# Banded attention and a mixture of experts in one kernel: larger loads of the plain heads, dealt out over the steps; half of the V shifts on VectorE; another opening; another PSUM pool for routing

## The chip, the cores and the metric

The kernel runs on one core of a Trainium2 chip. The metric is the device time of one execution in microseconds (us). Three runs of the kernel before gave 720.86, 727.56 and 734.02 us; their median is 727.56 us.

## The reference

```python
B, H, S, D = 8, 8, 576, 64          # batch, heads, sequence, head size
# attention: window 32; heads 0-3 "plain", heads 4-7 dilated by 4
rel = pos[:, None] - pos[None, :]
mask_plain = (rel >= 0) & (rel < 32)
mask_dil   = (rel >= 0) & (rel < 128) & (rel % 4 == 0)
attn = softmax(where(mask, q @ k.T / 8, -1e9));  out = attn @ v
x = out.transpose(0, 2, 1, 3).reshape(B * S, H * D)      # 4608 tokens x 512
# mixture of experts: one of 8 experts a token
logits = x @ w_gate + modality_bias[modality_id]
e = argmax(logits);  g = softmax(logits)[e]
out = g * (relu(x @ w1[e]) @ w2[e])                      # w1: 512 x 1024, w2: 1024 x 512
```

All data are float32.

## The kernel before

The kernel has two parts. The first runs over the eight batch elements ("batches" here) and computes attention and routing. The second, `slots`, runs the experts over slots of up to 256 tokens.

**Units and steps.** A batch is cut into nine units of 64 queries for each of four (head, block) pairs. Work is a software pipeline of 72 + 6 steps, written out by hand as the body of one loop over `t`; TensorE, VectorE, ScalarE and SyncE run in the order in which that code is written (`manual_schedule`), GpSimd in an order that is tied down too. A step is called b.m here: batch b, m-th step of the batch (t = 9b + m). Step t does, in this order: the scores of unit t and, on VectorE, mask and maximum (`sm`, `nmx`; GpSimd then subtracts); the exponential of unit t-1; one shift of V (`shift_v`, L148); the transposes of the probabilities of unit t-2 and of the result rows of unit t-5; one "chunk" of transposes that turn the next Q and K (`qk_chunks`, L332 for plain heads, L339 for dilated ones); probabilities times V of unit t-3 (`attend`, L427) and its normalisation on VectorE, which ends in the tile `x_sb` (L445); the gate logits of the unit before that; then, twice, a stage of the background tasks (`advance`), of which `gating` is the routing of a batch; then the store of finished `x_sb` to the DRAM tensors `x_dram` (`keep`, L458 to L468); and last the loads for later batches.

**What waits for what.** `x_sb` has three buffers, each filled by two units and freed when its store has landed. PSUM pool `o` has two buffers of one bank, from which `attend`, the logits and both matmul groups of `gating` (L549: turning the logits; L574 to L577: counting ranks) take turns. PSUM pool `two` has two buffers of two banks (`pw`) for all transposes.

**SyncE's queue.** All plain loads and stores are issued by SyncE, one after the other. In step b.2 it gets the loads of the next batch's plain K, in b.3 those of plain Q and dilated V, in b.7 dilated Q and K of the batch after, in b.8 plain V. `load_one` (L115) stages plain heads with six tokens of 64 a row on 2 x 48 rows: a DMA for each of four heads and two halves, eight for K and eight for Q, 73.7 KB each (48 rows x 6 tokens x 256 B). Stores go between them: one in each of b.1, b.3, b.5, b.7, three in b.8.

**Shifts.** The V tiles hold each block of 64 keys; their first 32 rows are the last 32 of the block before, copied on chip by `shift_v`: eight copies of 32 x 520 numbers a batch, in steps b.0 to b.7, all on ScalarE.

**Routing.** `gating` of batch b starts in step 5 of the batch after. For batch 2 it is followed by `slot_info`, by `fetch_slot` (loads of token lists, `idt`, L743) and by gathers on GpSimd (`xr`, L313, the helper line of all GpSimd work); these fill four early slots, so that the experts can start when the last unit's scores are done.

**Opening.** The first loads, before the loop, are put in order by a scheduler. Nine dummy matmuls (L180) run while they are under way.

Of the kernel before, what the change touches and what calls it, by code (L numbers as in the profile page):

```python
# [10 lines left out]
F32 = mybir.dt.float32  # L11
# [3 lines left out]
AF = mybir.ActivationFunctionType  # L15
# [3 lines left out]
ET = mybir.EngineType  # L19
# [8 lines left out]
WIN = 32  # L28
NCLS = 4
CL = S // NCLS  # L30
TQ = 64
# [3 lines left out]
PG = 64  # L35
SI = S // (2 * PQ)
GB = 96
NGB = S // GB
# [21 lines left out]
def kernel(  # L60
# [46 lines left out]

    def load_one(b, kd, src, queue=nc.sync):

        t = ald.tile([PG + PQ, SI * 4 * D], F32, name="st")  # L110
        if kd == 0:
            tv = t.rearrange("p (s h d) -> p s h d", h=4, d=D)
            for h in range(4):
                for e in range(2):
                    queue.dma_start(out=tv[PG * e:PG * e + PQ, :, 2 * (h % 2) + h // 2],  # L115
                                    in_=src[b, h].rearrange("(e p s) d -> e p s d", e=2, s=SI)[e])
            return tv
        tv = t.rearrange("p (h x) -> p h x", h=4)
        for e in range(2):
            queue.dma_start(out=tv[PG * e:PG * e + PQ], in_=by_parity(src, b)[e])  # L120
        return tv

    def load_qk(b, kd, queue=nc.sync):
        kn = load_one(b, kd, k)
        return load_one(b, kd, q, queue), kn

# [3 lines left out]
    def load_v(b, kd, part=slice(None)):  # L130

        t = vw(b, kd)
        if kd == 0:
            for a in range(2):
                nc.sync.dma_start(out=t[WIN:KW, 0:2 * NTILE, 1 + D * a:1 + D * (a + 1)],
                                  in_=v[b, 2 * a:2 * a + 2].rearrange("g (i p) d -> p (g i) d", p=TQ))
        else:
            vv = v[b, 4:8].rearrange("h (j c a) d -> c j h (a d)", c=2, a=2)
            for i, o, c, j, n in VPARTS[part]:
                nc.sync.dma_start(out=t[WIN + o:WIN + o + n, 4 * i:4 * i + 4, 1:1 + 2 * D], in_=vv[c, j:j + n])  # L140
        return t

    def shift_v(b, kd, n):

        t = vw(b, kd)
        i = NTILE * (n % 2) + 4 * (n // 2) if kd == 0 else 4 * n
        o = i + 1 if kd == 0 else i + 4
        nc.scalar.copy(out=t[0:WIN, o:o + 4].rearrange("p i d -> p (i d)"), in_=t[TQ:KW, i:i + 4].rearrange("p i d -> p (i d)"))  # L148

    first = [ald.tile([PG + PQ, SI * 4 * D], F32, name="st").rearrange("p (h x) -> p h x", h=4) for _ in range(2)]  # L150
    for n in range(SI // 2):
        for t, src, queue in zip(first, (q, k), (nc.scalar, nc.sync)):
            xs = slice(2 * D * n, 2 * D * (n + 1))
            for e in range(2):
                queue.dma_start(out=t[PG * e:PG * e + PQ, :, xs], in_=by_parity(src, 0)[e, :, :, xs])
    state = {('qk', 0, 1): tuple(first)}
    warm = cpool.tile([P, 512], BF16, name="warm")
# [9 lines left out]
    nc.vector.memset(hot, 0.0)  # L167
    nc.scalar.activation(out=hot, in_=hot, func=AF.Exp)
# [3 lines left out]
    state['v', 0, 1] = load_v(0, 1, slice(0, 2))  # L172
    state['qk', 0, 0] = load_qk(0, 0)
    load_v(0, 1, slice(2, None))
    state['v', 0, 0] = load_v(0, 0)
    ident = cpool.tile([P, P], F32, name="ident")
    make_identity(nc, ident)
    for _ in range(NWARM):
        pw = psum['o'].tile([P, 512], F32, name="po")
        nc.tensor.matmul(out=pw, lhsT=warm[:, 0:P], rhs=warm, start=True, stop=True)  # L180

# [142 lines left out]
    def qk_chunks(kd, qn, kn):  # L324


        def turn(n, src, is_q, pt):
            if kd == 0:
                for i in range(SI):
                    for e in range(2):  # L330
# [3 lines left out]
                return [((qT[0] if is_q else kT[0][:, :, WIN:])[:, n].rearrange("c (e x) -> c e x", e=2), pt[:, :, 0:SI * PQ])]  # L334
            off = 0 if is_q else 4 * PQ
            for h in range(4):
                for e in range(2):
                    rows = slice(PG * e, PG * e + PQ)
                    nc.tensor.transpose(out=pt[:, e, off + PQ * h:off + PQ * (h + 1)], in_=src[rows, h, 2 * D * n:2 * D * (n + 1)],  # L339
                                        identity=ident[rows, rows])  # L340
# [711 lines left out]
    for ch in qk_chunks(1, *state['qk', 0, 1]):  # L1052
        ch()
    state['qk', 1, 1] = load_qk(1, 1)

# [17 lines left out]
    for t in range(NU + LAG):  # L1073
# [12 lines left out]
        if t < NU:  # L1086
            if m == 0:
                state['lT', b] = gwk.tile([2 * LGP, S], F32, name="lT")
            if b + 1 < B:
                if m == 4:  # L1090
                    pieces = qk_chunks(1, *state['qk', b + 1, 1])
                elif m == 8:
                    pieces = qk_chunks(0, *state['qk', b + 1, 0])
            units.append(Unit(b, m0, [state['v', b, 0], state['v', b, 1]], state['lT', b]))
            units[t].scores()
        step()
# [19 lines left out]
        for x in kept:  # L1116
            x.keepT()
        for _ in range(2 if t == 3 else 1):
            if pieces:
                pieces.pop(0)()  # L1120
        step()

# [17 lines left out]
        if 0 <= t - 4 < NU:  # L1140
            units[t - 4].keep(nc.sync)
        if t < NU and b + 1 < B:

            if m == 2:
                state['k', 0] = load_one(b + 1, 0, k)
            elif m == 3:
                state['qk', b + 1, 0] = load_one(b + 1, 0, q), state['k', 0]
                state['v', b + 1, 1] = load_v(b + 1, 1)
            elif m == 7 and b + 2 < B:
                state['qk', b + 2, 1] = load_qk(b + 2, 1)  # L1150
            elif m == 8:
                state['v', b + 1, 0] = load_v(b + 1, 0)
        advance([*round_of, B - 1] if moe and t < NU else range(-1, B))
# [42 lines left out]
```

## Time and profile before

| | |
|---|---|
| runs | 720.86, 727.56, 734.02 us |
| profiled execution | 715.86 us; span of its trace 714.1 us |
| first mask of unit 0, first of batch 1, first of batch 7 | 13.41, 48.47, 231.45 us |
| first matmul of the experts | 260.09 us |
| TensorE, VectorE, ScalarE, GpSimd busy | 652.5, 478.5, 440.3, 251.8 us |

The times of the third and fourth row are starts from the span's beginning. The expert part, from 260 us on, keeps TensorE busy almost without a gap (100.00 of the 100 us from 500 to 600). The text below looks at the part ahead of it. A row of a table by stretches has: the stretch, its length, then for each engine the busy time and the number of its instructions, then the granted TensorE clock (1.00 is full), the mean busy share of the 16 DMA engines, and GB/s. A row of the timeline has start, duration, engine (a q behind it: its instruction queue, here DMA issues), line, operation, tiles, shape, count, and in brackets the idle time of the engine before it with what ended it.

### The profile page before, as it was taken

The numbers are of one execution on the slowest core, as the hardware profiler recorded it, in microseconds if no ns is written. First come the engines' busy times: TensorE is split into PE (matmuls) and PEld (weight loads), VectorE is DVE, ScalarE is ACT, GpSimd is POOL, SyncE is SP. The second block draws the span as 40 slices with busy tenths as digits, with TensorE's granted clock in tenths as the row PEclk, the third lists the DMA queues.
The fourth block names the chain that finished last, engine by engine and source line by source line (L and its number), as shares of the span: only waits on it lengthen the run. The fifth ranks groups of instructions, "written<-read, shape, count | busy, mean of one in ns | idle before, by whom it ended". The sixth has DMA issues, their size and how long they took to land. (4 is left out here: it accounts for less than half of the span.)

```text
span 714.1 us, 19778 instructions
## 1 busy us (share of the span) xinstructions
PE 652.5 (91%) x7237; PEld 566.8 (79%) x7237; DVE 478.5 (67%) x1165; ACT 440.3 (62%) x917; POOL 251.8 (35%) x322
## 2 busy tenths in 40 slices
PE   6698788796887989999999999999999999999994
PEld 4587677675765868888998989989999999989983
DVE  4277477676666666796667766676677766677662
ACT  4479589585866655555665666556655656656652
POOL 6223456344655554343332313332233322211110
PEclk9999699778889669999999999999999999999997
DMA  6885867858686961389594324862333315941460
GB/s 150 161 200 135 192 170 155 197 127 181 157 187 161 252 155 54 88 150 265 136 258 139 99 81 116 242 174 72 96 87 104 118 69 130 242 137 59 122 168 12
DMA packets 136327, 103.45 MB, mean 145 GB/s; under 512 B 68800, under 2 KB 114386, under 8 KB 136228
## 3 DMA queue, kind: packets, MB, share of 16 engines
q1 hardware_dynamic: 126804, 82.31, 47.2%
q0 software_dynamic: 8176, 19.26, 9.2%
q8 instruction: 58, 0.95, 0.6%
q10 hardware_dynamic: 1248, 0.59, 0.3%
q14 instruction: 41, 0.34, 0.2%
HBM read 127.52 MB, written 29.39 MB: 220 GB/s over the span
## 5 line engine op out<-in xcount | busy, mean ns | idle before, releaser
L989 PE MATMUL pt<-xh,w1l 128*128 128x256 f32 (+1 forms) x608 | 172.5, 284 | 2.8 <-DVE w1l L938 2.8
L989 PE MATMUL pt<-xh,w1h 128*128 128x256 f32 (+1 forms) x608 | 173.3, 285 | 1.0 <-ACT w1h L937 0.9
L989 PE MATMUL pt<-xl,w1h 128*128 128x256 f32 (+1 forms) x608 | 171.9, 283 | 0.0
L995 ACT ACTIVATE hh<-pt 128x256 fp32r<-128x256 f32 (+1 forms) x152 | 57.5, 379 | 155.6 <-PE pt L989 155.6
L938 DVE TENSOR_TENSOR w2l<-w2q,w2h 128x512 fp32r<-128x512 f32 x152 | 104.9, 690 | 45.5 <-ACT w2h L937 37.9
L989 PEld LDWEIGHTS pt<-xh,w1h 128*128 128x128 f32 x608 | 115.9, 191 | 9.7 <-ACT w1h L937 3.0
L313 POOL DMA_INDIRECT xr<-x_dram,idt x74 | 82.1, 1110 | 112.9 <-DMA x_slot<-xr 64.3
L989 PEld LDWEIGHTS pt<-xl,w1h 128*128 128x128 f32 x608 | 115.9, 191 | 5.9
L989 PEld LDWEIGHTS pt<-xh,w1l 128*128 128x128 f32 x608 | 116.4, 191 | 4.3 <-DVE w1l L938 4.3
L969 PE MATMUL py<-w2h,hh 128*128 128x512 f32 x296 | 118.7, 401 | 0.0
L969 PE MATMUL py<-w2h,hl 128*128 128x512 f32 x296 | 116.7, 394 | 0.0
L969 PE MATMUL py<-w2l,hh 128*128 128x512 f32 x296 | 115.5, 390 | 0.0
L996 DVE SCALAR_TENSOR_TENSOR hl<-pt,hh 128x256 fp32r<-128x256 f32 (+1 forms) x152 | 63.0, 415 | 76.0 <-ACT hh L995 75.9
L313 POOL DMA_INDIRECT out_dram<-ys,idt x37 | 40.4, 1091 | 200.4 <-ACT ys L972 120.6
L938 DVE TENSOR_TENSOR w1l<-w1q,w1h 128x512 fp32r<-128x512 f32 x152 | 104.4, 687 | 7.8 <-ACT w1h L937 7.7
L937 ACT CAST w1h<-w1q 128x512 fp32r<-128x512 f32 x152 | 94.6, 622 | 8.6 <-DMA w1q<-in_moe_w_dram 8.2
L937 ACT CAST w2h<-w2q 128x512 fp32r<-128x512 f32 x152 | 93.1, 612 | 0.0
L313 POOL TENSOR_TENSOR sm<-sm,nmx 128x384 f32<-128x384 f32 x72 | 60.0, 833 | 85.5 <-DVE nmx L397 43.8
L969 PEld LDWEIGHTS py<-w2l,hh 128*128 128x128 f32 x296 | 55.6, 188 | 13.8
L427 PE MATMUL po<-vw,pT 96*64 96x65 f32 (+1 forms) x1216 | 63.6, 253 | 0.4 <-DVE x_sb L445 0.4
L969 PEld LDWEIGHTS py<-w2h,hh 128*128 128x128 f32 x296 | 56.2, 190 | 7.7 <-issue 0.7
L969 PEld LDWEIGHTS py<-w2h,hl 128*128 128x128 f32 x296 | 55.6, 188 | 5.8
(178 smaller groups left out, 976.4 us busy)
## 6 DMA issues: line engine op xcount, KB each, us to landing
w2q<-in_moe_w_dram SPq DMA_DIRECT2D x76, 512.0 KB
w1q<-in_moe_w_dram SPq DMA_DIRECT2D x152, 256.0 KB
x_slot<-xr SPq DMA_DIRECT2D x18, 512.0 KB
xg<-x_slot SPq DMA_DIRECT2D x72, 128.0 KB
x_dram<-x_sb SPq DMA_DIRECT2D x32, 256.0 KB
vw<-in_v_dram SPq DMA_DIRECT2D x16, 288.0 KB
st<-in_k_dram SPq DMA_DIRECT2D x64, 72.0 KB
st<-in_q_dram SPq DMA_DIRECT2D x64, 72.0 KB
```

What stands on the lines that cost most here:

```text
L313: ins = tc.keep_in_program_order(getattr(nc.gpsimd, name)(*args, **kw))
L427: nc.tensor.matmul(out=pov[r0:r0 + nr, g, cs], lhsT=self.pT[:, 2 * g + a, r0:r0 + nr], rhs=self.vts[kd][:, blk, cs], start=True, stop=True)
L937: nc.scalar.copy(out=hi, in_=raw)
L938: nc.vector.tensor_tensor(out=lo, in0=raw, in1=hi.bitcast(F32), op=ALU.subtract)
L969: nc.tensor.matmul(out=py[u], lhsT=ht[:, us], rhs=wt, start=(f + n == 0), stop=(f + n == FC + 1))
L989: nc.tensor.matmul(out=ph, lhsT=wt[:, c, :], rhs=xt[:, c, 0:cols], start=(c + i == 0), stop=(c + i == KC + 1))
L995: nc.scalar.activation(out=hh, in_=ph, func=AF.Relu)
L996: nc.vector.scalar_tensor_tensor(out=hl, in0=ph, scalar=0.0, in1=hh.bitcast(F32), op0=ALU.max, op1=ALU.subtract)
```

## The change

**Plain heads.** They are staged with nine tokens a row on 64 rows, one head of a pair in the upper and one in the lower half of the partitions: a DMA a head, four for K and four for Q, 147.5 KB each. `turn` transposes 64 x 128 blocks: 10 in a first chunk and 8 in a second, for K and for Q, 36 a batch where there were 48. ScalarE's copy out of PSUM then writes runs of five or four numbers instead of one long run.

**Loads dealt out.** From batch 1 on the loads are issued in parts of one to three DMAs a step: K in b.0 and b.1, Q in b.2 and b.3, dilated V in b.3 to b.5, dilated K in b.6, dilated Q in b.7 and b.8, plain V in b.8 and the next step.

**Shifts.** Those with an odd number go to VectorE (steps b.1, b.3, b.5, b.7).

**Routing.** `loose()` takes a buffer of pool `two` where no chunk is left in the step (`state['loose']`), and one of pool `o` otherwise. The counting of ranks moves on by one background stage.

**Opening.** The order of its loads is fixed by hand: dilated Q and K, all of dilated V, plain K and Q, plain V. 21 more dummy matmuls (`fill`), of 64 rows, stand between the first chunks and units.

```diff
-    def load_one(b, kd, src, queue=nc.sync):
-        t = ald.tile([PG + PQ, SI * 4 * D], F32, name="st")
-        if kd == 0:
-            tv = t.rearrange("p (s h d) -> p s h d", h=4, d=D)
-            for h in range(4):
-                for e in range(2):
-                    queue.dma_start(out=tv[PG * e:PG * e + PQ, :, 2 * (h % 2) + h // 2],
-                                    in_=src[b, h].rearrange("(e p s) d -> e p s d", e=2, s=SI)[e])
-            return tv
...
+    def load_plain(t, b, src, heads, queue=nc.sync):
+        tv = t[:, 0:SP * 2 * D].rearrange("p (s a d) -> p s a d", a=2, d=D)
+        for h in heads:
+            queue.dma_start(out=tv[PG * (h % 2):PG * (h % 2 + 1), :, h // 2], in_=src[b, h].rearrange("(p s) d -> p s d", s=SP))
...
-        nc.scalar.copy(out=t[0:WIN, o:o + 4].rearrange("p i d -> p (i d)"), in_=t[TQ:KW, i:i + 4].rearrange("p i d -> p (i d)"))
+        move = nc.vector.tensor_copy if n % 2 else nc.scalar.copy
+        move(out=t[0:WIN, o:o + 4].rearrange("p i d -> p (i d)"), in_=t[TQ:KW, i:i + 4].rearrange("p i d -> p (i d)"))
...
+    with tc.manual_schedule(engines={ET.SP, ET.Activation}):
+        state['qk', 0, 1] = staged(), staged()
+        for xs in (slice(0, 2 * D), slice(2 * D, None)):
+            load_dil(state['qk', 0, 1][0], 0, q, range(2), xs, nc.scalar)
+            load_dil(state['qk', 0, 1][1], 0, k, range(2), xs)
+        nc.scalar.activation(out=hot, in_=hot, func=AF.Exp)
+        state['v', 0, 1] = load_v(0, 1)
...
+    def fill(n):
+        po = psum['o'].tile([P, 512], F32, name="po")
+        for _ in range(n):
+            nc.tensor.matmul(out=po, lhsT=warm[0:PG, 0:P], rhs=warm[0:PG], start=True, stop=True)
...
-                for i in range(SI):
-                    for e in range(2):
-                        rows = slice(PG * e, PG * e + PQ)
-                        nc.tensor.transpose(out=pt[:, e, i:SI * PQ:SI], in_=src[rows, i, 2 * n:2 * n + 2].rearrange("p a d -> p (a d)"),
+                s0, ns = (0, 5) if n == 0 else (5, SP - 5)
+                for i in range(ns):
+                    for g in range(2):
+                        rows = slice(PG * g, PG * (g + 1))
+                        nc.tensor.transpose(out=pt[:, g, i:ns * PG:ns], in_=src[rows, 2 * D * (s0 + i):2 * D * (s0 + i + 1)],
...
+    def loose():
+        if psum['two'] and state['loose']:
+            return psum['two'].tile([P, 2, 512], F32, name="pw")[:, 0]
+        return psum['o'].tile([P, 512], F32, name="po")
...
-        lgp = psum['o'].tile([P, 512], F32, name="po")
+        lgp = loose()
...
-        rkp = psum['o'].tile([P, 512], F32, name="po")
+        if b < B - 1:
+            yield
+        rkp = loose()
...
+        state['loose'] = not pieces
         for _ in range(2 if t == 3 else 1):
             if pieces:
                 pieces.pop(0)()
...
+            if m == 0 and b > 0:
+                load_v(b, 0, slice(1, 2))
+            if b + 1 < B:
...
+                if m < 4 and b > 0:
+                    load_plain(state['qk', b + 1, 0][m < 2], b + 1, k if m < 2 else q, (2 * (m % 2), 2 * (m % 2) + 1))
...
+                if 3 <= m < 6:
+                    state['v', b + 1, 1] = load_v(b + 1, 1, slice(2 * (m - 3), 2 * (m - 2)))
```

**SyncE, third batch.** In the queue before, from the store of step 2.1 to the loads of step 2.7 (`st` is the staging tile of Q and K, `vw` V, `x_sb` a finished result; the shapes are rows x tokens x numbers):

```order
L465 DMA x_dram_84<-x_sb 128x2x256
L115 DMA st<-in_k_dram 48x6x64 x8
L465 DMA x_dram_84<-x_sb 128x2x256
L115 DMA st<-in_q_dram 48x6x64 x8
L140 DMA vw_104<-in_v_dram 64x4x128 x2
L140 DMA vw_104<-in_v_dram 16x4x128
L140 DMA vw_104<-in_v_dram 48x4x128
L140 DMA vw_104<-in_v_dram 64x4x128
L140 DMA vw_104<-in_v_dram 32x4x128
L468 DMA x_dram_85<-x_sb 128x2x256 x2
L120 DMA st<-in_k_dram 48x4x384 x2
```

The same place after the change, from step 2.0 to step 2.5:

```order
L116 DMA st<-in_k_dram 64x9x64 x2
L469 DMA x_dram_84<-x_sb 128x2x256
L116 DMA st<-in_k_dram 64x9x64 x2
L116 DMA st<-in_q_dram 64x9x64 x2
L469 DMA x_dram_84<-x_sb 128x2x256
L116 DMA st<-in_q_dram 64x9x64 x2
L137 DMA vw_104<-in_v_dram 64x4x128 x2
L137 DMA vw_104<-in_v_dram 16x4x128
L137 DMA vw_104<-in_v_dram 48x4x128
L472 DMA x_dram_85<-x_sb 128x2x256
L137 DMA vw_104<-in_v_dram 64x4x128
L137 DMA vw_104<-in_v_dram 32x4x128
```

Between the store of step 2.3 (the second of the `x_dram_84` rows) and that of step 2.5 (`x_dram_85`) there were fourteen loads and are now six.

**TensorE, steps 1.6 and 1.8 after the change.** First the turning of the logits (`lT`), then the counting of ranks (`oh`, `upper`), each with what stands ahead of it:

```order
L343 MATMUL pw<-ident,st 128x48 x16
L431 MATMUL po<-vw_106,pT 64x65 x8
L512 MATMUL po<-ux,wgs 64x128 x2
L558 MATMUL po<-ident,lT 96x72 x6
L396 MATMUL pss<-kT_102,qT_100 64x96 x8
```

and, two steps on,

```order
L335 MATMUL pw<-ident,st 128x64 x10
L431 MATMUL po<-vw_104,pT 64x65 x8
L512 MATMUL po<-ux,wgs 64x128 x2
L585 LDWEIGHTS upper
L585 MATMUL po<-oh,upper 96x48
```

Both still write `po`, pool `o`, behind `attend` and the logits as before: a chunk (L343, L335) was waiting at the head of both steps, so `state['loose']` was false. The same holds for the batches after it, but for one group, L558 of batch 6 in step 7.6, which writes `pw`.

**GpSimd, steps 4.8 to 5.1.** Before (`xr` is a gather of rows by the list `idt`, `table` a scatter, `t_...` and `run` small routing operations):

```order
L313 TENSOR_TENSOR run<-run,r_3660 96x8 x3
L313 TENSOR_TENSOR t_3657<-t_3657,oh 96x48
L313 TENSOR_TENSOR sm<-sm,nmx 128x384
L601 DMA table<-pay,dst 41472x3
L313 DMA xr<-x_dram_84,idt 128x256
L313 TENSOR_TENSOR sm<-sm,nmx 128x384
L313 DMA xr<-x_dram_85,idt 128x256
```

After:

```order
L315 TENSOR_TENSOR run<-run,r_3575 96x8 x3
L315 TENSOR_TENSOR sm<-sm,nmx 128x384
L315 TENSOR_TENSOR t_3572<-t_3572,oh 96x48
L612 DMA table<-pay,dst 41472x3
L315 TENSOR_TENSOR sm<-sm,nmx 128x384
L315 DMA xr<-x_dram_84,idt 128x256
L315 DMA xr<-x_dram_85,idt 128x256
```

The first gather now stands one subtraction (`sm`), that is one step, later, and the routing product `t` behind the subtraction instead of ahead of it.

More of the change, by code (lines that the diff above doesn't have):

```diff
@@ L36 @@
 SI = S // (2 * PQ)
+SP = S // PG
 GB = 96
@@ L133, in load_v @@
         if kd == 0:
-            for a in range(2):
+            for a in range(2)[part]:
                 nc.sync.dma_start(out=t[WIN:KW, 0:2 * NTILE, 1 + D * a:1 + D * (a + 1)],
@@ L147, in shift_v @@
         o = i + 1 if kd == 0 else i + 4
[L148 to L156, printed above, removed]
+        move = nc.vector.tensor_copy if n % 2 else nc.scalar.copy
+        move(out=t[0:WIN, o:o + 4].rearrange("p i d -> p (i d)"), in_=t[TQ:KW, i:i + 4].rearrange("p i d -> p (i d)"))
     warm = cpool.tile([P, 512], BF16, name="warm")
@@ L167 @@
     nc.vector.memset(hot, 0.0)
-    nc.scalar.activation(out=hot, in_=hot, func=AF.Exp)
     for kd in (1, 0):
@@ L171 @@
     nc.vector.memset(kT[1][:, :, WIN + HP:], 0.0)
[L172 to L175, printed above, removed]
+    state = {}
+    with tc.manual_schedule(engines={ET.SP, ET.Activation}):
[5 more added lines that the diff above has]
+        state['v', 0, 1] = load_v(0, 1)
+        state['qk', 0, 0] = staged(), staged()
+        load_plain(state['qk', 0, 0][1], 0, k, range(4))
+        load_plain(state['qk', 0, 0][0], 0, q, range(4))
+        state['v', 0, 0] = load_v(0, 0)
     ident = cpool.tile([P, P], F32, name="ident")
     make_identity(nc, ident)
-    for _ in range(NWARM):
-        pw = psum['o'].tile([P, 512], F32, name="po")
-        nc.tensor.matmul(out=pw, lhsT=warm[:, 0:P], rhs=warm, start=True, stop=True)
+    def fill(n):
+        po = psum['o'].tile([P, 512], F32, name="po")
+        for _ in range(n):
+            nc.tensor.matmul(out=po, lhsT=warm[0:PG, 0:P], rhs=warm[0:PG], start=True, stop=True)
+    fill(NWARM)
     starts = [None, 0, CL - 2 * TQ]
@@ L338, in turn @@
                     rows = slice(PG * e, PG * e + PQ)
-                    nc.tensor.transpose(out=pt[:, e, off + PQ * h:off + PQ * (h + 1)], in_=src[rows, h, 2 * D * n:2 * D * (n + 1)],
+                    nc.tensor.transpose(out=pt[:, e, off + PQ * h:off + PQ * (h + 1)], in_=src[rows, SI * D * h + 2 * D * n:SI * D * h + 2 * D * (n + 1)],
                                         identity=ident[rows, rows])
@@ L1053 @@
         ch()
-    state['qk', 1, 1] = load_qk(1, 1)
+        fill(3)
+    state['qk', 1, 1] = staged(), staged()
+    load_dil(state['qk', 1, 1][1], 1, k, range(2))
+    load_dil(state['qk', 1, 1][0], 1, q, range(2))
     credit = 0.0
@@ L1094 @@
             units.append(Unit(b, m0, [state['v', b, 0], state['v', b, 1]], state['lT', b]))
+            if t in (1, 2):
+                fill(2)
             units[t].scores()
@@ L1120 @@
                 pieces.pop(0)()
+        if t < 4:
+            fill(2)
         step()
@@ L1141 @@
             units[t - 4].keep(nc.sync)
[L1142 to L1152, printed above, removed]
+        if t < NU:
+            if m == 0 and b > 0:
+                load_v(b, 0, slice(1, 2))
+            if b + 1 < B:
+                if m == (0 if b > 0 else 2):
+                    state['qk', b + 1, 0] = staged(), staged()
+                if m < 4 and b > 0:
+                    load_plain(state['qk', b + 1, 0][m < 2], b + 1, k if m < 2 else q, (2 * (m % 2), 2 * (m % 2) + 1))
+                elif m in (2, 3):
+                    load_plain(state['qk', b + 1, 0][m < 3], b + 1, k if m < 3 else q, range(4))
+                if 3 <= m < 6:
+                    state['v', b + 1, 1] = load_v(b + 1, 1, slice(2 * (m - 3), 2 * (m - 2)))
+                if m == 8:
+                    state['v', b + 1, 0] = load_v(b + 1, 0, slice(0, 1))
+            if b + 2 < B:
+                if m == 6:
+                    state['qk', b + 2, 1] = staged(), staged()
+                    load_dil(state['qk', b + 2, 1][1], b + 2, k, range(2))
+                elif m > 6:
+                    load_dil(state['qk', b + 2, 1][0], b + 2, q, (m - 7,))
         advance([*round_of, B - 1] if moe and t < NU else range(-1, B))
```

16 lines of the change are left out of this document (8 added, 8 removed).

## The prediction

> **What bounds the kernel now.** I read the page first, for where TensorE is not full:
>
> ```profile
> PE   6698788796887989999999999999999999999994
> ...
> PEclk9999699778889669999999999999999999999997
> ```
>
> A slice is 17.9 us. From the 16th on TensorE is full: the experts, which the change leaves alone. Ahead of it there are gaps and, in about half of the slices, a clock below full. Next the table by stretches, once for each batch (cut at the starts of L394, the mask of a batch's first unit, and counting that line alone):
>
> ```profile
> 13.41:48.47 35.06, 4.98 (x9) 1.00 0.74 169
> 48.47:77.57 29.10, 4.94 (x9) 0.96 0.74 166
> ...
> 231.45:260.09 28.64, 4.92 (x9) 0.68 0.91 212
> ```
>
> Nine units take 29 to 35 us (28.64 in the last batch, which has no loads for a next one). What could they take? Two stretches without a stall, one at full clock, one at half (first all engines: TensorE, its weight loads, VectorE, ScalarE, GpSimd; then L394 alone):
>
> ```profile
> 48.48:63.31 14.83, 14.23 (x380) 11.80 (x374) 12.13 (x38) 14.47 (x31) 4.96 (x6) 1.00 0.85 174
> 48.48:63.31 14.83, 3.29 (x6) 1.00 0.85 174
> 135.82:150.80 14.98, 2.20 (x4) 0.53 0.81 166
> ```
>
> Six units in 14.83 us are 2.47 us each, with TensorE 96% and ScalarE 98% busy; at half clock four take 14.98 us, 3.75 us each. Half clock costs 1 - 2.47/3.75 = 34% of its time. Nine good steps would be 22 us. The rest of each batch is stalls and half clock, and the timeline shows what makes both:
>
> ```profile
> 66.40 0.55 PE L549 MATMUL po<-ident,lT 72*96 72x72 f32 x6 [0.80 <-DVE x_sb L445]
> ...
> 69.07 3.72 SPq L140 DMA_DIRECT2D vw<-in_v_dram  x6
> ...
> 72.88 0.90 SPq L468 DMA_DIRECT2D x_dram<-x_sb  x2
> ...
> 75.29 0.42 DVE L445 TENSOR_TENSOR x_sb<-po,den 128x256 f32<-128x256 f32 x1 [3.35 <-DMA x_dram<-x_sb]
> ...
> 75.86 0.25 PE L574 MATMUL po<-oh,upper 96*96 96x48 bf16 x1 [4.20 <-DVE x_sb L445]
> ```
>
> SyncE comes to the store L468 of step 1.5 only at 72.88, behind its row of loads. The normalisation of step 1.8 needs that buffer, waits until 75.29, and holds `po`, so TensorE waits 4.20 us. Right behind such gaps the granted clock is half:
>
> ```profile
> 75.00:88.60 13.60, 12.74 (x211) 11.03 (x211) 7.75 (x27) 7.62 (x15) 5.64 (x7) 0.50 0.94 185
> 133.00:150.00 17.00, 16.19 (x258) 13.71 (x258) 11.08 (x45) 9.06 (x19) 9.15 (x11) 0.50 0.84 170
> 228.60:245.60 17.00, 15.88 (x251) 13.49 (x251) 9.80 (x33) 8.49 (x17) 6.84 (x9) 0.50 0.98 250
> 174.00:184.10 10.10, 4.97 (x76) 4.02 (x78) 2.87 (x8) 5.54 (x12) 7.43 (x8) 0.50 0.57 140
> 204.70:211.40 6.70, 6.70 (x110) 5.65 (x111) 3.63 (x10) 3.75 (x8) 2.36 (x4) 0.50 0.59 161
> ...
> PE po L574 <- DVE x_sb L445: 13.6, 6, 4.2
> ```
>
> The first three follow the gap shown and its like in batches 4 and 7; the last row is the wait's total, six times. So the path of the first part is SyncE's queue, then `x_sb`, `po`, and the clock.
>
> **The change part by part**, against 715.86 us (span 714.1 and 1.76 around it).
>
> *SyncE's queue.* Plain Q and K are 16 issues, now 8. A plain issue's price:
>
> ```profile
> 50.59 1.39 SPq L135 DMA_DIRECT2D vw<-in_v_dram  x2
> ...
> 55.57 5.95 SPq L115 DMA_DIRECT2D st<-in_k_dram  x8
> ```
>
> 0.74 us each for 73.7 KB, 0.70 for 295 KB (L135), so I take 0.7 for the new 147.5 KB: 8 x 0.7 = 5.6 us less a batch. More important is the order: between the stores of b.3 and b.5 stood 14 issues, about 10 us or four steps; now 6, 4.2 us in two steps of 2.47. The store of b.5 then goes out in b.5, three steps (7.4 us) before its buffer is wanted. The L574 waits fall to the 0.8 that the `po` buffer costs anyway (as at L549): 13.6 - 6 x 0.8 = **-8.8**, bounds 0 and -8.8. Routing itself still takes `po` in all but one case (the order in the section above), so the 0.8 stays.
>
> *The clock.* Without those gaps 13.6 + 17.0 + 17.0 us at half clock would run in 66%: -16.2. The third has its DMA engines at 0.98, loading expert weights, so I count half of it: **-13.3**, bounds 0 and -16.2.
>
> The Trainium skill ("TensorE: Matmul & The Clock Gate", Part 1: The HAM clock gate) has the clock fall after an idle window of some 3.4 us. The row 204.70 speaks against so long a window: the gap ahead of it was
>
> ```profile
> 204.59 0.40 PE L505 MATMUL po<-ux,wgs 128*64 128x32 f32 x4 [1.99 <-issue]
> ```
>
> 1.99 us. By the page a change without 3.4 us gaps would be at full clock all through, and the sum 2.3 us lower. By the row 2 us are enough, so I keep this stretch (6.7 x 34% = 2.3 us) and do not take it off.
>
> *The first gather.*
>
> ```profile
> 167.95 3.41 SPq L743 DMA_DIRECT2D idt<-table  x2
> ...
> 175.22 1.05 POOL L313 DMA_INDIRECT xr<-x_dram,idt  x1 [5.26 <-DMA st<-in_k_dram]
> ...
> 179.13 0.66 PE L414 MATMUL pw<-ident,pe 64*96 64x64 f32 x8 [5.45 <-ACT ux L495]
> ```
>
> GpSimd waits 5.26 us for a list issued at 167.95, its subtractions with it, and TensorE 5.45 us; 10.1 us of half clock follow (3.4 us lost). The gather now comes one step later against the list, so about half of the wait goes: (5.45 + 3.4) / 2, **-4**, bounds 0 and -8.9.
>
> *The opening.*
>
> ```profile
> 1.27 4.02 PE L180 MATMUL po<-warm 128*128 128x512 bf16 x9 [1.27 <-DVE warm L158]
> ...
> 22.63 0.62 ACT L148 COPY vw<-vw 32x520 f32<-32x520 f32 x1 [4.88 <-DMA vw<-in_v_dram]
> ...
> 23.78 0.66 PE L414 MATMUL pw<-ident,pe 64*96 64x64 f32 x8 [4.74 <-ACT pT L420]
> ...
> 34.47 0.92 PE L392 MATMUL pss<-kT,qT 64*64 64x96 f32 x16
> ...
> 49.81 0.56 PE L392 MATMUL pss<-kT,qT 64*64 64x96 f32 x16
> ...
> 15.00:30.00 15.00, 9.47 (x142) 7.70 (x142) 5.79 (x15) 7.79 (x14) 3.85 (x6) 1.00 0.73 154
> ```
>
> A shift waits for V behind 16 plain loads: 4.74 us, gone with V ahead of them. Eight issues of 0.7 us less bring all later loads 5.6 us forward. Equal work takes 0.92 us at 34.47 and 0.56 at 49.81: batch 0 runs cold whatever the clock column says there. The dummy matmuls (4.02/9 = 0.45 us, 21 are 9.4 us) keep TensorE busier; they lie in its idle time (5.5 of these 15 us, and in the wait for the first loads), and cost some 3 us where they don't. Bounds: -4 (the V wait alone, with the fill in the way) and -12.5 (nine units of 2.47 us); **-9**.
>
> *Shifts on VectorE.*
>
> ```profile
> L148 ACT COPY vw<-vw 32x520 f32<-32x520 f32 x64 | 39.9, 623 | 6.4 <-DMA vw<-in_v_dram 4.9
> 35.34 0.17 DVE L280 CAST ewt<-ewt_i 96x48 f32<-96x48 int32 x1
> ...
> 35.52 0.20 DVE L288 CAST placef<-place 96x96 f32<-96x96 int32 x1
> L394 DVE TENSOR_TENSOR sm<-pss,masks 128x384 f32<-128x384 f32 x72 | 39.6, 550 | 23.0 <-PE pss L392 17.6 <-ACT pe L402 5.0
> L313 POOL TENSOR_TENSOR sm<-sm,nmx 128x384 f32<-128x384 f32 x72 | 60.0, 833 | 85.5 <-DVE nmx L397 43.8 <-DVE den L434 20.4 <-ACT ux L495 13.3
> ```
>
> Of 64 copies of 0.623 us, 32 leave ScalarE. On VectorE 48 more numbers cost 0.03 us (0.17 to 0.20), so 520 cost about 0.17 + 472 x 0.0006 = 0.46 us; by L394, 550 ns for 384, at most 0.75. VectorE has (14.83 - 12.13)/6 = 0.45 us free in a good step: the copy just fits, ahead of the normalisation. If it did not fit, 32 x 0.46 to 32 x 0.75 = 15 to 24 us. For it: ScalarE, 98% busy, loses 0.62 us in every second step, which lets it keep up with TensorE's 96% (at best 72 x 0.1 = -7). I take **0**, bounds -7 and +24.
>
> The Trainium skill speaks against it ("SBUF — State Buffer", Who interferes with whom): a copy of VectorE in its two-port mode and an operation of GpSimd lock each other out. No row here shows a VectorE copy of this size beside GpSimd; the price is in the rivals.
>
> *Chunks.* 48 transposes with 48 columns and 36 with 64 are both 2304 columns: 0. ScalarE writes shorter runs; strided copies of 384 numbers took as long as plain ones of 576:
>
> ```profile
> 25.84 0.64 ACT L353 ACTIVATE qT<-pw 128x576 f32<-128x576 f32 x1
> ...
> 33.52 0.69 ACT L353 ACTIVATE qT<-pw 128x384 f32<-128x384 f32 x1 [2.05 <-PE pw L339]
> ```
>
> At that rate (1.8 against 1.1 ns a number) 2304 numbers a batch cost 0 to +1.6 us; with ScalarE relieved I take 0.25 x 8 = **+2**.
>
> Sum: -8.8 - 13.3 - 4 - 9 + 0 + 2 = -33, or 683 us on the profiled execution. This lies 11.7 us below the median of the runs. Waits of this kind are what can differ between runs, and the change takes them out, so I carry over little of that: **684 us**.
>
> **Rivals.**
> (a) Gaps come up elsewhere and half of the half-clock terms stays: with gaps of 0.8 us in two steps of each batch, and 1.99 us known to be enough, that is easy. -33 becomes -20: 696, up to 705.
> (b) The lock: the copy stands right behind `nmx`, where GpSimd's subtraction starts. If each of 32 copies waits out one of 0.833 us, 26.7 us come back: 684 + 27 = 711. It decides once the wait passes VectorE's 0.45 us of room. This is the rule as a mechanism of this kernel (the Trainium skill, same section); nothing in the trace bears on it yet.
> (c) DMA is the bound: 0.74 x 29.1 = 21.5 us of a batch are DMA time already. Against it: the stretch at 2.47 us a unit ran at 0.85. If batches stay at 28 us: about 700.
> (d) The stores still land late, behind loads in the DMA engines rather than in SyncE's queue. Then only the opening and the chunks pay: 716 - 7, and against the median 715.
> (e) Slower: steps that VectorE now bounds leave TensorE so idle that the clock stays half throughout. 72 x 3.75 = 270 us in place of 246.7 (13.41 to 260.09): +23, 739 to 751. It decides where idle time nears 2 us in 3.4; in a 2.9 us step with 2.4 of TensorE it is 0.5, which speaks against it.
>
> **How the numbers follow.** Forecast 0.58 (own range 666 to 694), (a) 0.17, (b) 0.08, (c) 0.05, (d) 0.08, (e) 0.04. The range 665 to 712 reaches over (a), (b) and (c) and leaves out (d), (e) and the tails. A measurement of this kernel can tell about 2%: under 713.0 us is faster. That is the forecast, (a), (c) and most of (b), 0.86; within 2% 0.10, from (d) and the rest; slower 0.04, (e).
>
> **What would show it.** Right: no `x_sb` waiting for `x_dram` and no L574 gap over 1 us; first masks of batches 1 and 7 near 39 and 200 us, the experts' first matmul near 227; clock column above 0.95 in batches 1 to 6. Wrong: VectorE copies of 0.8 us or more, or with a wait ahead of `den` (b); DMA share over 0.95 in every batch (c); store waits as before with SyncE idle (d); clock 0.5 in steps without a gap (e).

## The result

The changed kernel takes 709.32 us (median of 4 runs, 700.49 to 715.69; a fifth took 704.17); the kernel before 725.07 (4 runs, 720.86 to 734.02). The ratio is 0.971, with a 95% interval of 0.962 to 0.979. Ratios and intervals compare only runs close to the fastest of their kernel, here 700.49, 703.07 and 704.17 us with 720.86, 722.58 and 727.56, so that 0.971 stands for 21 us where the medians differ by 16. Run again on another chip the change took 692.10 (688.66 to 704.91, 6 runs) against 717.87: 0.964, interval 0.957 to 0.971. So it is faster by 2.9 and 3.6%, 16 and 26 us by the medians, where the forecast was 684, 44 below the median then known (727.56): the direction was right, the size too large. The 709.32 lies in the stated range of 665 to 712, but near its end and outside the forecast's own 666 to 694: it falls in the range because the rivals had been given room there. The 692.10 lies in the forecast's own range.

The profiled execution of the change, 715.69 us, is the longest of its runs; that of before, 715.86, is shorter than every other run of it in that round. The two traces are therefore of equal length, and the difference in the medians has to be looked for in what varies between executions.

### The profile page after: what moved, and what is told of

The parts are those of the page before. It is cut to its first block, busy times and chain, and to the rows that moved or that the text cites. A ratio compares the mean times of both kernels' runs of the same rounds, so it can differ in the third digit from the quotient of the medians.

```text
span 714.0 us, 19541 instructions
## 1 busy us (share of the span) xinstructions
PE 669.3 (94%) x7162; PEld 572.6 (80%) x7162; DVE 491.7 (69%) x1197; ACT 421.7 (59%) x885; POOL 255.7 (36%) x322
## 5 line engine op out<-in xcount | busy, mean ns | idle before, releaser
L315 POOL TENSOR_TENSOR sm<-sm,nmx 128x384 f32<-128x384 f32 x72 | 64.8, 900 | 97.9 <-DVE nmx L401 71.6
L431 PE MATMUL po<-vw,pT 96*64 96x65 f32 (+1 forms) x1216 | 69.4, 262 | 5.8 <-issue 3.2
L424 ACT COPY pT<-pw 96x512 f32<-96x512 f32 x69 | 39.7, 575 | 53.2 <-PE pw L492 43.2
L431 PEld LDWEIGHTS po<-vw,pT 96*64 96x64 f32 (+1 forms) x1216 | 56.5, 163 | 14.5 <-issue 6.1
```

The source lines that it names most:

```text
L315: ins = tc.keep_in_program_order(getattr(nc.gpsimd, name)(*args, **kw))
L424: nc.scalar.copy(out=self.pT.rearrange("p j (u c) -> p j u c", u=2) if two else self.pT, in_=self.pt)
L431: nc.tensor.matmul(out=pov[r0:r0 + nr, g, cs], lhsT=self.pT[:, 2 * g + a, r0:r0 + nr], rhs=self.vts[kd][:, blk, cs], start=True, stop=True)
```

## The profile after

The page of the changed kernel, its row for TensorE, and TensorE and its granted clock in 40 slices:

```profile
span 714.0 us, 19541 instructions
...
PE 669.3 (94%) x7162; PEld 572.6 (80%) x7162; DVE 491.7 (69%) x1197; ACT 421.7 (59%) x885; POOL 255.7 (36%) x322
...
PE   8998889899898889889999999999999999999994
...
PEclk9999968767679899999999999999999999999997
```

The holes of before (the 6s and 7s in the PE row) are filled. Yet the clock column is worse in six of the seven slices from the sixth to the twelfth (and better in the fifth, 14th and 15th), and TensorE is busy for 669.3 us, 16.8 more than before (652.5), with 75 matmuls fewer (96 fewer transposes, 21 more dummies). In this execution, what it no longer waits, it works more slowly.

The waits of TensorE from 15 to 260 us (total, times, longest):

```profile
PE po L585 <- DVE x_sb L449: 4.8, 6, 1.3
PE po L558 <- DVE x_sb L449: 4.2, 6, 0.8
```

The first was 13.6 us in six waits of up to 4.2. No `x_sb` waits for a store in this trace, and the 5.26 us wait of the first gather is gone too. By batches, cut at the mask of the first unit (L398) and counting that line alone; the last columns are granted clock, DMA share, GB/s:

```profile
15.17:48.43 33.26, 4.99 (x10) 1.00 0.84 187
48.43:72.82 24.39, 4.95 (x9) 1.00 0.86 194
72.82:103.53 30.71, 4.93 (x10) 0.81 0.83 172
103.53:135.75 32.22, 4.94 (x10) 0.75 0.68 144
135.75:172.28 36.53, 4.99 (x10) 0.67 0.63 134
172.28:206.88 34.60, 4.96 (x10) 0.70 0.71 154
206.88:232.58 25.70, 4.90 (x10) 0.99 0.79 193
232.58:259.24 26.66, 4.84 (x9) 0.82 1.01 227
```

At full clock a batch takes 24.39 (batch 1) and 25.70 us (batch 6), against 29.1 and 32.6 before. Batches 2 to 5 are at 0.67 to 0.81 and take 30.7 to 36.5. What stands ahead of such a stretch is now small:

```profile
88.35 0.56 PE L396 MATMUL pss<-kT,qT 64*64 64x96 f32 x16
...
89.98 0.70 PE L343 MATMUL pw<-ident,st 48*128 48x48 f32 x16 [0.56 <-ACT kT L359]
...
92.33 0.93 PE L558 MATMUL po<-ident,lT 72*96 72x72 f32 x6 [0.81 <-DVE x_sb L449]
```

The clock fell at 92.14 and stayed at half until 105.80. Ahead of it lie 0.56 us of waiting for ScalarE's evacuation of a chunk and the greater part of 0.81 us for the buffer of routing, no gap of 2 us. In four such stretches TensorE is nearly always busy (the columns are TensorE, its weight loads, VectorE, ScalarE, GpSimd, then clock):

```profile
92.14:105.80 13.66, 12.96 (x183) 10.64 (x183) 7.37 (x25) 6.68 (x16) 4.09 (x10) 0.50 0.82 154
119.45:133.10 13.65, 12.87 (x182) 10.38 (x183) 7.82 (x25) 6.32 (x17) 3.78 (x7) 0.50 0.58 129
146.76:170.65 23.89, 23.04 (x332) 18.40 (x331) 15.39 (x57) 13.43 (x30) 7.36 (x13) 0.50 0.53 124
184.31:204.78 20.47, 19.87 (x306) 16.40 (x297) 12.01 (x37) 12.39 (x30) 10.22 (x14) 0.50 0.70 142
```

That gave the theory for the experiments: the gain is taken back by half clock, and half clock comes with ordinary waits that leave TensorE idle for about a third of 3.4 us, whatever their single length. The rivals: the copies on VectorE or GpSimd's operations beside them set the pace; or a part of the change costs what another brings.

## The experiments

Twelve runs on four chips, each timed against the kernel before on the same chip. Its medians there: 721.62 beside shifts, loads in rows, old opening and first fills; 726.39 beside old routing, layout alone and second fills; 728.22 beside layout and dealing, without and with fills or two-bank routing; 717.87 beside the last pair. Runs of one kernel spread over 3 to 27 us, so a median of four is good to some 4 us (an estimate).

### One part undone at a time

Shifts on ScalarE again:

```diff
-        move = nc.vector.tensor_copy if n % 2 else nc.scalar.copy
-        move(out=t[0:WIN, o:o + 4]...
+        nc.scalar.copy(out=t[0:WIN, o:o + 4]...
```

> The changed kernel with all 64 shift copies on ScalarE again (32 fewer copies of 0.42 us on VectorE, 32 more of 0.62 us on ScalarE). Theory (the gain was lost to stretches at half clock, which follow 3.4 us in which TensorE is busy under about two thirds): ScalarE is the engine that TensorE waits for in the steps with chunks, so 0 to +20 us against the 709 of the change, and the half-clock stretches stay. Rival (the copies on VectorE, and GpSimd's subtraction beside them at 0.90 instead of 0.83 us, gave the gain back): 685 to 699, 10 to 24 us less.

711.85 us (697.17 to 715.64; no interval was given). By the medians the copies on VectorE neither gave nor took anything that can be told. What they cost shows in the changed kernel's groups (busy, mean ns):

```profile
L146 ACT COPY vw<-vw 32x520 f32<-32x520 f32 x32 | 20.0, 623 | 0.8
...
L146 DVE COPY vw<-vw 32x520 f32<-32x520 f32 x32 | 13.5, 422 | 1.0
...
L315 POOL TENSOR_TENSOR sm<-sm,nmx 128x384 f32<-128x384 f32 x72 | 64.8, 900 | 97.9 <-DVE nmx L401 71.6
```

0.42 us each, and GpSimd's subtraction goes from 833 to 900 ns; with the shifts on ScalarE again it is back at 832. That is 72 x 0.067 = 4.8 us, or 0.15 us for each of the 32 copies, on an engine that is busy for 36% of the span.

Loads in rows again (K at step 2, Q and all V parts at step 3, dilated Q and K at step 7, plain V at step 8):

```diff
-                if m < 4 and b > 0:
-                    load_plain(..., (2 * (m % 2), 2 * (m % 2) + 1))
...
+            if m == 2:
+                load_plain(state['qk', b + 1, 0][1], b + 1, k, range(4))
+            elif m == 3:
+                load_plain(state['qk', b + 1, 0][0], b + 1, q, range(4))
+                state['v', b + 1, 1] = load_v(b + 1, 1)
```

> The changed kernel with its loads issued in rows again as before the change (K at step 2, Q and all six V parts at step 3, dilated Q and K at step 7, plain V at step 8), in the new layout of 8 issues for plain Q and K. Theory: the dealing is what removed the waits of the store behind the row; with six V issues and four Q issues in one step, about 7 us, a wait on x_sb of 1 to 3 us comes back in each batch, and the time is 709 + 3 to + 12. If half as many issues were enough: 709 +/- 4.

710.10 us (703.52 to 718.20), ratio 0.983, 0.974 to 0.991. The `x_sb` wait that was expected in each batch came back once, 2.4 us, and TensorE's waits at the rank rose from 4.8 to 8.4 us. The dealing alone moves no time that these runs can tell.

The opening of before, in the new layout:

```diff
-    with tc.manual_schedule(engines={ET.SP, ET.Activation}):
-        for xs in (slice(0, 2 * D), slice(2 * D, None)):
...
-        state['v', 0, 1] = load_v(0, 1)
+    state['v', 0, 1] = load_v(0, 1, slice(0, 2))
     state['qk', 0, 0] = staged(), staged()
     load_plain(state['qk', 0, 0][1], 0, k, range(4))
     load_plain(state['qk', 0, 0][0], 0, q, range(4))
+    load_v(0, 1, slice(2, None))
...
-        fill(3)
...
-                fill(2)
```

> The changed kernel with the opening of before (first tiles in three pieces, two of the V parts, plain K and Q, the other V parts; nine dummy matmuls at the start and none later), in the new layout. Theory: the first masks of batch 1 came at 48.4 us with the new opening and 48.5 with the old one, so 709 +/- 4. My forecast took 9 us for the new opening: by it 718.

710.12 us (702.94 to 717.03), ratio 0.978, 0.971 to 0.985. Its batch 1 began at 45.5 us, against 48.4 with the new opening, and the clock came up at 43.9 instead of 47.8. In the other traces of the new layout (the two with fills at the chunks aside) batch 1 begins at 44.0 to 45.8 us with the old opening and at 46.0 to 48.4 with the new. The new opening costs some 2 to 3 us at that place; the end of the program does not show it.

Routing as before (always `po`, the rank one step of the generator earlier):

```diff
-        if b < B - 1:
-            yield
-        rkp = loose()
+        rkp = psum['o'].tile([P, 512], F32, name="po")
```

> The changed kernel with routing as before the change: both of its tiles always from the pool of one-bank buffers, and the rank one step earlier. In the changed kernel all but one of these tiles came from that pool anyway, so what is undone is the later step of the rank. Theory: the rank's matmuls then stand behind the transposes' step again and wait for x_sb, 1 to 2 us longer a batch: 709 + 4 to + 12. If it is worth nothing: 709 +/- 4.

709.65 us (705.75 to 711.54), ratio 0.981, 0.972 to 0.990. No waits came back that were not there (5.1 us at the rank, six times). At full clock the time from the first mask of a batch to its second took 2.65 us here and 2.99 in the changed kernel (medians of five), but batch 1 as a whole, at full clock in both, 24.46 and 24.39: the later rank costs nothing that can be told.

### The layout alone

All four of these parts undone; what stays is nine tokens a row, eight issues instead of sixteen for plain Q and K. Against the kernel before:

```diff
-            for h in range(4):
-                for e in range(2):
-                    queue.dma_start(out=tv[PG * e:PG * e + PQ, :, 2 * (h % 2) + h // 2], ...
+        for h in heads:
+            queue.dma_start(out=tv[PG * (h % 2):PG * (h % 2 + 1), :, h // 2], ...
```

> The kernel before with the plain heads staged nine tokens a row alone: half as many plain Q and K issues, 36 transposes with 64 columns in place of 48 with 48. Loads in rows, the opening, all shifts on ScalarE and routing as before. Undoing the dealing (710.1), the opening (710.1) or the shifts (711.9) one at a time cost at most 3 us beside the 709 to 710 of the change. Theory: the eight issues fewer a batch are what took the long waits away, so 708 to 716. Rival (each part is enough by itself, and the gain is lost only when all are undone): 718 to 725 here.

710.60 us (700.52 to 716.30) against 726.39: -15.8, as much as the whole change gave in its first round (no interval was given). First the wait of `x_sb` in the kernel before, then three waits of this one:

```profile
DVE x_sb L445 <- DMA x_dram<-x_sb: 8.8, 3, 3.3
...
PE po L572 <- DVE x_sb L443: 8.3, 6, 4.1
PE po L547 <- DVE x_sb L443: 6.5, 7, 1.7
...
DVE x_sb L443 <- DMA x_dram<-x_sb: 2.6, 1, 2.6
```

One late store instead of three. Its trace is 15.4 us shorter than that of before (698.7 and 714.1); it has 44.4 us of half clock after 48 us where before has 78.5, which at 34% is 11.6 us, and its batch 1 begins 3.5 us earlier (44.99 and 48.48). As an estimate these two make up the difference. The layout changes the issues and the transposes at once, and no run parts them: that the eight issues fewer did it fits the waits, but is not shown.

So each part undone alone (ratios 0.978 to 0.983 where an interval was given) and all four undone measure the same as each other, to what these runs can tell, and those intervals overlap with the change's, 0.962 to 0.979.

Layout and dealing together: the changed kernel with the edits above to shifts, opening and routing, and none to the loads:

> The changed kernel without three of its parts: shifts on ScalarE, the opening and routing as before; what stays is the new layout and the dealing of the loads. The layout alone gave 710.6 us, and its x_sb still waited once for a late store (2.6 us), which held TensorE 4.1 us. Theory: the dealing takes that wait away too, but what is left is set by the half clock, which comes with ordinary gaps: 700 to 711. Rival (the dealing is worth the 8 to 22 us forecast for waits and clock, and the other parts took it back): 685 to 699.

701.45 us (694.71 to 706.69) against 728.22, ratio 0.955, 0.945 to 0.965. That is the fast end of what the theory gave. The kernel before spread widest on this chip: the ratio fits a mean of 730 us for it, without its two shortest runs (710.85 and 721.44), and by the medians it would be 0.963. The time lies 8 us under the changed kernel's first round, but on another chip, and the interval overlaps with that of the change in both rounds. The opening would be some 3 to 4 us of the 8 (batch 1 begins at 44.04 us); whether the rest is chance is not settled.

### Dummy matmuls against half clock

First attempt, dummy transposes into the step's PSUM tile, written after its evacuations in the program:

```diff
+    for _ in range(n):   # 3 ahead of a chunk, 6 ahead of a routing tile
+        nc.tensor.matmul(out=state['both'][:, 0, 6 * TQ:], lhsT=ident, rhs=ident, start=True, stop=True)
```

> The changed kernel with dummy transposes of 128 columns (about 0.1 us each at full clock) ahead of every chunk (3) and ahead of the two places where routing takes a PSUM buffer (6), into columns that nothing reads: some 15 us of work, most of it in gaps of TensorE. Theory: the clock column rises to about 1.00 in batches 2 to 6, batches 2 to 5 (30.7 to 36.5 us) fall toward 25 to 28, and the time falls by 10 to 24 us, to 685-699, although the program has more work. Rival (VectorE and GpSimd set the pace): the batches stay at 30 us or more whatever the clock is, and the time is 705 to 725. Rival (the clock does not follow TensorE's busy share): the half-clock stretches stay, and the fills cost 5 to 15 us, 714 to 724.

820.52 us, ratio 1.135, 1.124 to 1.145. This told nothing on the theories, since the fills had a wait of their own:

```profile
PE pw L554 <- ACT ux L499: 52.6, 43, 3.8
```

The fills wrote other columns of the step's tile, and still waited for the evacuation of the rest. Second attempt, ahead of the evacuations:

```diff
+        if pieces and both is not None and 4 <= t < NU:   # 2 of 128 columns
+            nc.tensor.matmul(out=both[:, 0, 6 * TQ:], lhsT=ident, rhs=ident, start=True, stop=True)
         for x in kept:
             x.keepT()
...
             turned[t - LAG].logits(lo)
+            if both is not None and t < NU and m in (6, 8):   # 3 of 120 columns
+                nc.tensor.matmul(out=lo[:, LG0 + P:], lhsT=ident, rhs=ident[:, 0:512 - LG0 - P], start=True, stop=True)
```

> The fills of the earlier run again, but written behind the step's own transposes and ahead of its evacuations in the program, so that they wait for no evacuation: 2 dummy transposes (0.22 us each by the earlier run) ahead of each step's chunk, 3 of 120 columns ahead of the two places a batch where routing takes a buffer; 26 us of dummy work in all, some 20 of it into gaps. Theory: half clock comes from TensorE's busy share in a 3.4-us window, so the clock column stays at 1.00 nearly throughout batches 1 to 7, and the batches take 25 to 28 us each: 685 to 700. Rival (other engines set the pace, the clock is not what is lost): batches as in the changed kernel or longer, 709 to 730. Rival (the clock follows something else): the half-clock stretches stay near 75 us, and 715 to 735.

722.71 us (710.03 to 736.92, 11 runs), ratio 0.989, 0.981 to 0.996: slower than the change, while the clock rose (mean of the runs 0.972; 0.944 for the change). The trace shows both. Stretches and groups:

```profile
95.91:99.32 3.41, 1.71 (x37) 1.26 (x32) 2.41 (x7) 1.48 (x3) 1.45 (x3) 1.00 0.88 184
99.32:126.63 27.31, 27.31 (x319) 22.47 (x321) 10.95 (x36) 11.62 (x26) 6.69 (x13) 0.50 0.42 91
...
152.70:184.40 31.70, 29.68 (x606) 23.91 (x604) 24.49 (x94) 20.63 (x44) 15.17 (x22) 1.00 0.72 153
184.40:216.50 32.10, 29.42 (x599) 24.06 (x597) 22.01 (x71) 20.25 (x44) 19.31 (x26) 1.00 0.76 172
```

```profile
L1134 PE MATMUL pw<-ident 128*128 128x128 f32 x196 | 38.1, 321 | 0.0
L1156 PE MATMUL po<-ident 128*128 128x120 f32 x90 | 16.8, 332 | 0.0
```

From 126.63 to 259.75 the clock was full without a break, and batches 4 and 5 took 31.7 and 32.1 us with the fills in them, where the changed kernel's took 36.5 and 34.6 without. But the 286 fills sum to 54.9 us of TensorE, twice the 26 expected, and batch 1, at full clock in both, went from 24.39 to 28.32. The time is the one of the first rival (709 to 730), but batch 1 without fills shows that the other engines allow 24.39 us. Fills can keep the clock up over long stretches, though not throughout (27.31 us of half clock remained at 99 us, and as much from 259.75 on); at the chunks they cost more than they bring. So the half of the theory on the clock held in part, and its price did not.

Fills only at the two waits of routing, on the kernel with layout and dealing:

> The kernel with layout and dealing, plus dummy transposes at the two places a batch alone where routing waits for its buffer (3 each, 0.2 us apiece), no others. The run with fills at every chunk kept full clock from 127 to 260 us, with four batches at 29.1 to 32.1 us against 25.7 to 36.5, but its fills took their own 4 us a batch where TensorE was the bound. Theory: here the fills lie in gaps of 0.8 us that are waits anyway, busy shares of the windows with routing rise from 0.6 to 0.75, and there is less half clock: 690 to 705, at least 5 below the run without fills beside it. Rival (a clock at full speed does not pay, or the fills do not keep it): equal to the run without fills, or up to 5 us more.

695.07 us (694.61 to 697.91), ratio 0.952, 0.944 to 0.959: 6.4 us under the same kernel without fills (701.45), mean clock 0.959 against 0.938. It is the lowest ratio of all, though the intervals of the two overlap, and the remark on this chip's runs of before holds here too. The same on the changed kernel, and the changed kernel beside it:

> The changed kernel with dummy transposes only at its two waits of routing in each batch (3 each, 0.2 us apiece). With layout and dealing alone they took 701.5 to 695.1. Theory: the same here, less half clock, 6 to 12 us under the changed kernel beside it. Rival (the 6 us were chance, or hold only where ScalarE has the shifts): no difference, +/- 4 us.

> The changed kernel itself once more, beside the next run on the same chip, so that the two compare. 705 to 712, as before. If layout and dealing alone (701.5) are faster by more than chance, this is above 705; if the other three parts cost nothing, it is about 701.

690.68 us with fills (687.67 to 697.78), ratio 0.963, 0.956 to 0.970, and 692.10 without: 1.4 us, nothing that can be told, where 6 to 12 were expected. The changed kernel itself, expected at 705 to 712 or about 701, came out lower than both. The mean clock was 0.976 and 0.965: there was little half clock left to take away in that round.

### Routing in two-bank buffers throughout

On the kernel with layout and dealing:

```diff
+        if psum['two']:
+            return psum['two'].tile([P, 2, 512], F32, name="pw")[:, 0]
```

> The kernel with layout and dealing, and both tiles of routing from the pool of two-bank buffers in every batch but the last, which the change did in one case only. Theory: routing then waits for no normalisation, the gaps of 0.6 to 0.8 us ahead of its transposes and its rank go (some 9 us in all), and windows with a low busy share become fewer: 690 to 706. Rival (the next step's transposes wait for the buffer instead): 705 to 715.

701.79 us (697.66 to 707.73), ratio 0.959, 0.951 to 0.968: the same as without (701.45). The wait moved, as the rival said, though the time did not rise to its 705 to 715:

```profile
PE pw L329 <- ACT ux L493: 7.5, 5, 1.6
```

The next step's chunk now waits for the buffer.

### The same program twice

The changed kernel's second trace (691.01 us, on another chip; the same instructions) is the best evidence on where the gain went. Its page, batches 2 to 5, and two of its waits:

```profile
PE 643.7 (93%) x7162; PEld 553.5 (80%) x7162; DVE 491.1 (71%) x1197; ACT 420.9 (61%) x885; POOL 257.5 (37%) x322
...
PEclk9999989967999999999999999999999999999997
```

```profile
72.55:99.95 27.40, 4.90 (x9) 0.97 0.88 198
99.95:127.15 27.20, 4.90 (x10) 0.91 0.67 155
127.15:160.34 33.19, 4.97 (x10) 0.73 0.73 155
160.34:188.36 28.02, 4.90 (x9) 0.95 0.84 179
...
PE po L585 <- DVE x_sb L449: 6.6, 6, 2.5
...
DVE x_sb L449 <- DMA x_dram<-x_sb: 1.5, 1, 1.5
```

VectorE, ScalarE and GpSimd are as busy as in the first trace to 2 us; TensorE's 7162 matmuls take 25.6 us less, and the program 24.7 us less. Batches 2 to 5 take 115.8 us instead of 134.1, with 27.3 us of half clock in them instead of 71.7. The other 6.4 us are the experts: from their first matmul to the end of the span 448.3 us on this chip against 454.7. (The kernel before is some 8 us faster on it too than on the other three, at the same mean clock.) So two executions of one program, on two chips, differ by as much as the change gains; 44.4 us less half clock at 34% would be 15 of the 24.7 us, as an estimate.

## Why the prediction was right, and where not

**The direction** rested on the stalls at SyncE's queue and on the clock, and both moved. The kernel before shows a mean granted clock of 0.906 (39 runs), the change 0.944 in its first round and 0.965 in its second. As an estimate, with half clock on twice the missing share and 34% of that time lost: 0.188 x 724 x 0.34 = 46 us before, 0.112 x 708 x 0.34 = 27 and 0.070 x 694 x 0.34 = 17 after. The differences, 19 and 30, are the size of the measured 16 and 26.

That the gain is one of the clock nearly alone does not follow from this, for three reasons. Among the 39 runs of before, a clock higher by 0.01 goes with 2.2 us less (fitted within each chip, standard error 0.5), not with the 4.9 of this formula; at 2.2 the clock would be 8 of the 16 us and 13 of the 26. The mean clock is also rough: in eleven of the fourteen traces its record begins only when the clock first changes, at 42 to 48 us (79 in one), and counts as full what lies ahead; in the three where it begins earlier, 31 to 34 us of half clock lie there, 0.02 of the mean. And as an estimate from the traces, with 34% of the half clock between 48 us and the experts taken off, the experts would start at 236.6 us before and at 231.4 and 229.3 in the two traces of the change: 5 to 7 us that the clock does not explain. So how much of the gain is the clock stays open: about half by the fit, nearly all by the formula. It varies from one execution to the next.

**SyncE's queue (-8.8): right as a wait.** 13.6 us became 4.8 (6.6 in the second trace), and `x_sb` waits for no store (once, 1.5 us, in the second trace). Put down to the wrong half, as far as time goes: I called the order of the loads more important than their number. In waits the layout alone brought 13.6 to 8.3, and the dealing undone raised 4.8 to 8.4, so both take part. In time the layout gave the whole first round's gain, and the dealing undone cost nothing that can be told.

**The clock (-13.3): this is the step that failed.** It said that half clock would go with the long gaps it followed, so that three stretches of 13.6, 17.0 and 17.0 us would run in 66% of their time. The gaps went, but the first trace of the change has 85 us of half clock after 48 us, where before had 78; the second has 34. What half clock followed was not the long gap alone: it also followed 3.4 us in which short waits left TensorE busy for two thirds, and the sum priced none of those. Rival (a), gaps that come up elsewhere, is what happened, in the first round beyond its 696 to 705. (Its 696 leaves out the whole -13.3; half of it would have given some 690. And the gaps ahead of the three stretches stand in batches 1, 3 and 6 in the numbering of the steps, not 4 and 7.) I had also taken for the base a trace with the clock at 0.94, when the runs of before average 0.906; this error goes the other way and hid part of the first. "I carry over little" of the 11.7 us between that trace and the median was a guess, and it stood for the term that mattered.

**The first gather (-4): right that the wait goes, not why.** Both waits of over 5 us are gone. But with routing as before, where the gather stands where it stood, GpSimd waits 0.30 us ahead of it, and with the layout alone 1.73: the later place was not needed. That the list now leaves SyncE's queue early enough is the likely reason, and no run tests it. In the second trace, where the clock was 0.95, batch 5 takes 28.0 us against 33.0 before; in the first, at 0.70, 34.6.

**The opening (-9): wrong, it gave nothing.** Batch 1 begins at 48.4 us, before at 48.5. The V wait is gone and the loads come earlier, and that is worth 3 us by the layout alone (45.0), but the fills take it back: the first two steps take 2.59 and 3.35 us where they took 1.60 and 2.52. The clock comes up at 47.8, later than before (44.2); in two other traces with the new opening it came up at 41.9 and 42.1, so this varies. That batch 0 runs cold was right, and three traces with the old opening show it in a row such as this:

```profile
13.10:45.00 31.90, 5.00 (x10) 0.53 0.90 201
```

This is the layout alone. Why keeping TensorE busier there does not reliably lift the clock earlier is open.

**Shifts (0): right**, with 0.42 us for the estimate of 0.46. Rival (b), the lock, costs 0.15 us of GpSimd's time for each copy, not 0.83 of VectorE's. In its own form it shows once in the 256 copies of the eight traces that have them: at 170.03 us of the second trace a copy took 1.44 us beside a subtraction and GpSimd's scatters; no other took over 0.53. **Chunks (+2): right** as work of ScalarE: the four evacuations of a batch take 2 x (0.77 + 0.67) = 2.88 us where four of 0.64 were 2.58, 2.4 us in all; the two rows of K:

```profile
L359 ACT COPY kT<-pw 128x640 f32<-128x640 f32 x8 | 6.1, 767 | 0.7 <-PE pw L335 0.7
L359 ACT COPY kT<-pw 128x512 f32<-128x512 f32 x8 | 5.4, 670 | 0.0
```

Of the signs to look for, "no L574 gap over 1 us" and the `x_sb` waits came true or nearly (the longest was 1.3, and 2.5 in the second trace); "batch 7 near 200, the experts near 227, clock over 0.95 in batches 1 to 6" did not: 232.6 and 259.2 in the first trace, 215.3 and 240.9 in the second. "Clock 0.5 in steps without a gap", which I had set as the sign of (e), appeared without (e): the time did not become longer, since batches 1 and 6, at or near full clock, took 24.39 and 25.70 us where they had taken 29.1 and 32.6.

## What to carry to other kernels

When a trace shows TensorE at half clock, do not price its return by the longest gap ahead of it: look at the share of each 3.4 us in which TensorE is busy, and ask whether the change lifts all of them over about three quarters. Take the granted clock of all runs, not of the one with a profile, as the base of a forecast. Profile one program more than once before a gain is explained: here two executions differed by as much as the change gained. Of a change in five parts, one may bring the gain: here the layout, probably by its fewer DMA issues in front of a store, and the rest measured nothing by itself.

## What the runs showed of the hardware

All changes of the clock lie on a grid of 3.413 us. Counted over all 14 traces, 50 to 330 us, for each interval of that grid at full clock, by the share in which TensorE was busy in it, how often half clock followed:

```
busy under 0.525     39 of  40
0.525 to 0.725       41 of 114
over 0.725            1 of 751
```

An idle interval is not needed: the fall at 92.14 us followed an interval in which TensorE was busy for 0.66 of it, between waits of 0.56 and 0.81 us. These are counts of what followed what; no run set the busy share by itself. The Trainium skill ("TensorE: Matmul & The Clock Gate", Part 1: The HAM clock gate) asks for an idle window, which these counts contradict; its section "A second HAM failure mode: psum-queue depth-cycling", by which short idle times between groups make the clock swing, agrees with them, and I had passed over it.

The way back is not one busy interval either. After an interval with TensorE busy for 0.98 or more of it, full clock returned in 80 of 169 cases, after one with less than that never (80 cases). Stretches last 3.1 intervals on average, 10.5 us, up to ten; in the run with fills at the chunks two lasted 27.31 us, one of them with TensorE busy all through. What decides it is not shown by these traces.
